# Agent attention and a top-1 mixture on one core: the first queries as f16 pairs among the keys, program order up to the first layer, and the last count of strays made early

## The chip, the cores and the metric

The kernel runs on one core of a Trainium2 chip. The metric is the device time of one execution in microseconds (us), from fast executions; the median of three runs stands for the kernel. One further execution was taken with a hardware profiler, and every row shown here comes from it. Engines are named as the profile names them: PE (matmuls), PEld (its weight loads), DVE (vector), ACT (scalar), POOL (GpSimd), SP (the queue that issues most DMAs).

## The reference

Attention through 49 agents per batch, then a mixture of 8 experts in which each token goes to the expert of its largest logit:

```python
# B, N, C = 4, 11456, 128; 49 agents; E, F = 8, 1024
a2k = softmax(scale * agents @ k.T)          # over the 11456 keys
agent_v = a2k @ v                            # 49 x 128
q2a = softmax(scale * q @ agents.T)          # over the 49 agents
x = (q2a @ agent_v).reshape(B * N, 128)

logits = normed(x) @ normed(expert_emb).T / tau
e = argmax(logits)
out = probs[e] * (relu(x @ w1[e]) @ w2[e])
```

Inputs and output are float32.

## The kernel before

**Units.** The tokens of a batch are laid out in 90 columns of (up to) 128. A unit is 8 columns: 128 partitions x 8 x 128 numbers, 512 KB, one load; a batch has 12 units (u = 0 to 11), the last of two columns of 96. Units of keys are kt, of values vt, of queries qt.

**The first batch's stages**, ahead of the first layer of the mixture:
- *Keys* (k1_f32). Each unit is transposed on PE in float32 (fTp, L362, 8 matmuls), copied out in halves by ACT and DVE (fT), multiplied with the agents (sp, L380, 8 matmuls, each run in two passes, 16 records), kept scaled as s_u by ACT (L383), and DVE keeps a running maximum m_run (L339).
- *Column maximum* (k_max, allmax): DVE reduces m_run to m, PE transposes it (mT, L149) and spreads the maximum (mB, L154), ACT copies it to pm.
- *Values* (k2_unit). DVE subtracts pm from s_u (kd, L398), ACT takes the exponential in place (L400), PE multiplies with the values (avp, L406), DVE adds up (avx, L412).
- *Fold and pick* (av_chain, pick_expert). PE folds the sums, the batch's main expert e0i is found (L487), SP reads it as a number (L545) and loads that expert's w1s and w2s (load_expert), which ACT and DVE turn into f16 pairs (gh, gl, w2h, w2l).

**Queries** (q_unit) need scores, DVE's maximum qmx and difference qe, ACT's exponential, and an f16 pair (high and low part) of the weights e that is transposed to tt; tt times r_hi and r_lo gives the router's sums (rtp), and tt feeds the mixture. Units 0 and 1 of the first batch are worked in float32 on PE (L566, and L588 for the transposes of e). All others go through split: ACT squares the unit for a scale (L299), DVE makes the scale out of it in three small operations (L179 to L183), ACT writes the high part (L303), POOL scales (L304) and subtracts for the low part (L305), SP issues a DMA transpose (L307), and PE takes 24 f16 matmuls (L316 to L318). Keys of later batches (k1_unit) go through split too.

**The mixture.** 736 steps (4 batches x 23 tiles x 8 slices of F): two matmuls of the first layer (hp, L723 and L724), ReLU and low part (hh on ACT, hl on DVE), twelve of the second (yp), then the output tile ot (L760). Beside it the next batch's keys and values and all queries are worked. Tokens whose expert is not e0 are strays: they are marked per batch, counted (count_strays: the maximum over partitions by mT, mB and pm, then running sums cum on DVE), and redone one group at a time. One group is redone beside the last batch (stray_first); at the end the count runs again, left over groups are computed (left, lefti), a register is loaded from lefti (L1097), and a loop runs over what is left.

**Order.** The generators run in rounds of a step counter, and each writes its instructions as it is reached; a number yielded is a wait in rounds. What the program writes is then placed by a scheduler on each engine, except that in the stages ahead of the first layer SP keeps the program's order (manual_schedule). k_max, av_chain and pick_expert run at high priority. In first, ops lists the units: 12 key units, two query units, the maximum, 12 value units, with two query units (u = 2, 3) and the next batch's first two key units set in between (BETWEEN); loads run AHEAD = 8 units ahead. Engine queues are in order: an instruction that waits holds up all behind it on its engine.

## Time and profile before

| what | value |
|---|---|
| runs | 1103.6, 1105.27, 1106.59 us (median 1105.27) |
| profiled execution | 1101.58 us, its span 1099.8 us |
| granted TensorE clock over the span | 0.973 of 2.4 GHz |
| PE busy | 1019.3 us, 93% of the span |
| DVE, ACT, POOL busy | 770.5, 724.2, 580.1 us |
| keys of the first batch | 0 to 46.6 us |
| maximum, first queries | 46.6 to 57.2 us |
| values | 57.2 to 84.25 us |
| fold, pick, weights | 84.25 to 101.2 us |
| mixture | 101.2 to 1094 us |
| count and end | 1094 to 1099.8 us |

Busy time is the union of an engine's instructions; an engine that is busy may still not be the one that sets the end. Start times count from the span's start. In a timeline row the bracket gives the idle time of the engine just before, and the instruction on whose end the idle time ended. A row of several instructions of the same kind ends in their count.

### The profile page before, as it was taken

To read this page: it belongs to the slowest core of one execution; us is meant where nothing else is said; L and a number is where in the kernel's file an instruction comes from. 1 tells how busy PE (TensorE), PEld (TensorE's weight loads), DVE (VectorE), ACT (ScalarE), POOL (GpSimd) and SP (SyncE) were. 2 spreads that over 40 slices of the span, in tenths; PEclk is the share of its full clock that TensorE was granted. 3 is DMA by queue.
4 is the path that set the end of the run, shared out by engine and by line. 5 is a ranking of instruction groups with operands and counts; after the bars stand their busy time and mean duration, and the time that the engine had idled before them with its cause. 6 is when DMAs were issued, how large, how long until landed. Compare 5 with 4: busy or idle time off the path is not lost.

```text
span 1099.8 us, 33877 instructions
## 1 busy us (share of the span) xinstructions
PE 1019.3 (93%) x13878; PEld 809.8 (74%) x13878; DVE 770.5 (70%) x1779; ACT 724.2 (66%) x1406; POOL 580.1 (53%) x653
## 2 busy tenths in 40 slices
PE   7876979999998898999999988999999989999997
PEld 7764767777776777777777766777777767877776
DVE  5665757666786677766686766766677778777785
ACT  3456978777559787766648866675556856755553
POOL 2334998786516987764524985544321835532300
PEclk9777999999999999999999999999999999999999
DMA  9549899956339988744436997452113524631101
GB/s 335 151 100 280 182 227 233 229 167 119 85 66 282 231 189 188 167 117 89 94 82 225 224 229 144 92 110 69 31 41 138 100 61 119 123 83 40 42 30 35
DMA packets 283944, 152.63 MB, mean 139 GB/s; under 512 B 208315, under 2 KB 260619, under 8 KB 283787
## 3 DMA queue, kind: packets, MB, share of 16 engines
q1 hardware_dynamic: 270603, 126.98, 51.2%
q10 hardware_dynamic: 13120, 23.47, 5.9%
q8 instruction: 109, 1.79, 0.7%
q14 instruction: 48, 0.39, 0.1%
q0 software_dynamic: 64, 0.00, 0.0%
HBM read 75.80 MB, written 23.53 MB: 90 GB/s over the span
## 4 chain that ended last, share of the span: by engine, by line
PE 53%; DMA 13%; POOL 13%; issue 9%; ACT 6%; DVE 5%; SPq 1%; ACTq 0%; POOLq 0%; DVEq 0%
PE hp L723 9%; PE yp L745 8%; PE yp L747 8%; PE hp L724 8%; PE yp L746 8%; DMA kT<-ks 4%; DMA tt<-e 4%; PE avp L406 4%; DMA qt<-in_q_dram 3%; POOL qs L305 2%; POOL qt L304 2%; POOL ks L305 2%; ACT hh L727 2%; POOL kt L304 2%; PE sp L380 2%
## 5 line engine op out<-in xcount | busy, mean ns | idle before, releaser
L728 DVE SCALAR_TENSOR_TENSOR hl<-hp,hh 128x512 f16<-128x512 f32 (+1 forms) x736 | 480.8, 671 | 142.5 <-ACT hh L727 121.7
L727 ACT ACTIVATE hh<-hp 128x512 f16<-128x512 f32 (+1 forms) x736 | 416.8, 588 | 186.1 <-PE yp L746 78.8
L745 PE MATMUL yp<-w2h,hh 128*128 128x128 f16 (+1 forms) x2880 | 522.4, 220 | 9.1 <-ACT hh L727 8.1
L746 PE MATMUL yp<-w2l,hh 128*128 128x128 f16 (+1 forms) x2880 | 521.7, 220 | 0.7 <-DVE w2l L532 0.7
L747 PE MATMUL yp<-w2h,hl 128*128 128x128 f16 (+1 forms) x2880 | 521.0, 220 | 0.0
L745 PEld LDWEIGHTS <-hh 128*128 128x128 f16 (+1 forms) x2880 | 285.3, 99 | 63.3 <-ACT hh L727 12.8
L747 PEld LDWEIGHTS <-hl 128*128 128x128 f16 (+1 forms) x2880 | 285.0, 99 | 47.2 <-issue 1.1
L746 PEld LDWEIGHTS <-hh 128*128 128x128 f16 (+1 forms) x2880 | 285.0, 99 | 42.1 <-issue 3.7
L723 PE MATMUL hp<-tt,gh 128*128 128x512 f16 (+1 forms) x736 | 275.9, 375 | 22.4 <-DVE hl L728 21.2
L724 PE MATMUL hp<-tt,gl 128*128 128x512 f16 (+1 forms) x736 | 276.0, 375 | 0.0
L304 POOL TENSOR_TENSOR qt<-qt,hsc 128x1024 f32<-128x1024 f32 (+1 forms) x46 | 81.8, 1781 | 49.6 <-ACT qs L303 42.9
L724 PEld LDWEIGHTS <-gl 128*128 128x128 f16 x736 | 72.0, 98 | 31.3 <-issue 28.7
L305 POOL TENSOR_TENSOR qs<-qt,qs 128x1024 f16<-128x1024 f32 (+1 forms) x46 | 92.0, 2004 | 0.4
L304 POOL TENSOR_TENSOR kt<-kt,hsc 128x1024 f32<-128x1024 f32 (+1 forms) x36 | 64.4, 1788 | 31.2 <-ACT ks L303 31.1
L723 PEld LDWEIGHTS <-gh 128*128 128x128 f16 x736 | 72.2, 98 | 8.5 <-issue 5.9
L650 POOL TENSOR_SCALAR l<-rtg 128x16 f32<-128x16 f32 (+2 forms) x28 | 8.2, 293 | 133.1 <-ACT rtg L615 132.4
L583 POOL TENSOR_TENSOR e<-qe,e 128x392 f16<-128x392 f32 (+1 forms) x46 | 39.7, 863 | 69.4 <-ACT e L582 58.7
L305 POOL TENSOR_TENSOR ks<-kt,ks 128x1024 f16<-128x1024 f32 (+1 forms) x36 | 72.8, 2022 | 0.6
L299 ACT ACTIVATE qs<-qt 128x1024 f16<-128x1024 f32 (+1 forms) x46 | 46.3, 1008 | 35.5 <-DMA qT<-qs 14.7
L648 POOL TENSOR_TENSOR nrm<-quad,half 128x16 f32<-128x16 f32 (+2 forms) x28 | 68.2, 2434 | 1.8
L406 PE MATMUL avp<-vt,kd 128*64 128x129 f32 x720 | 62.1, 297 | 6.5 <-issue 4.3
L760 DVE TENSOR_TENSOR ot<-yp,gs 128x512 f32<-128x512 f32 (+1 forms) x92 | 61.4, 670 | 9.6 <-PE yp L747 8.8
(264 smaller groups left out, 1452.7 us busy)
## 6 DMA issues: line engine op xcount, KB each, us to landing
kt<-in_k_dram SPq DMA_DIRECT2D x44, 512.0 KB, 5.9
qt<-in_q_dram SPq DMA_DIRECT2D x44, 512.0 KB, 6.2
vt<-in_v_dram SPq DMA_DIRECT2D x44, 512.0 KB, 5.2
out_dram<-ot ACTq DMA_DIRECT2D x88, 256.0 KB, 2.4
w1s<-in_moe_w_dram SPq DMA_DIRECT2D x5, 512.0 KB, 3.9
w2s<-in_moe_w_dram SPq DMA_DIRECT2D x5, 512.0 KB, 4.9
qT<-qs SPq DMA_TRANSPOSE x46, 5.0
tt<-e SPq DMA_TRANSPOSE x46, 3.5
```

The costliest lines, as they stand in the source:

```text
L304: pool.tensor_tensor(out=s[:p, :n], in0=s[:p, :n], in1=sc.unsqueeze(2).broadcast_to([p, n, D]), op=ALU.mult)
L305: pool.tensor_tensor(out=xs[:p, :n, 1], in0=s[:p, :n], in1=xs[:p, :n, 0], op=ALU.subtract)
L406: pe.matmul(out=avp[hs, :W], lhsT=de[:p, c * A : c * A + LO], rhs=src[:p, c, :], start=(c < 2), stop=(c >= n - 2), skip_group_check=True)
L648: pool.tensor_tensor(out=nrm, in0=quad[:, :n], in1=half[:, :n], op=ALU.pow)
L723: pe.matmul(out=hp[:, :m], lhsT=bt.gh[:, fs], rhs=tt, start=True, stop=False)
L724: pe.matmul(out=hp[:, :m], lhsT=bt.gl[:, fs], rhs=tt, start=False, stop=True)
L727: act.activation(hh[:, :m], hp[:, :m], AF.Relu)
L728: dve.scalar_tensor_tensor(out=hl[:, :m], in0=hp[:, :m], scalar=0.0, in1=hh[:, :m], op0=ALU.max, op1=ALU.subtract)
L745: pe.matmul(out=y, lhsT=hh[:, cs], rhs=bt.w2h[:, f, :], start=(f == 0 and c == 0), stop=False, skip_group_check=True)
L746: pe.matmul(out=y, lhsT=hh[:, cs], rhs=bt.w2l[:, f, :], start=False, stop=False, skip_group_check=True)
L747: pe.matmul(out=y, lhsT=hl[:, cs], rhs=bt.w2h[:, f, :], start=False, stop=last, skip_group_check=True)
L760: dve.tensor_tensor(out=o[:p, :n], in0=yp[:p, :n], in1=gate, op=ALU.mult)
```

## The change

It has five parts.
- **Queries 0 to 3 go through split**, among the keys: query unit 0 ahead of key unit 2, 1 ahead of 3, 2 ahead of 4, 3 ahead of 5 (QAT). The float32 way of the queries is gone. Weights e of all four are transposed by DMA (tt) and their low part is made by POOL.
- **In split, ahead of the mixture, the low part of a key unit** is one DVE operation in place of two on POOL, and there is a wait (5 rounds for queries, 1 for keys) ahead of the DMA transpose.
- **The next batch's key units 0 and 1** stand after value units 3 and 5 (KAT), not 8 and 11; AHEAD is 7; some waits in rounds are other numbers, and first also waits for these two units before av_chain.
- **Program order** up to the first layer holds for SP, PE, ACT and DVE, and high_priority is dropped there.
- **The last count of strays** with left and lefti is written in stray_first, as soon as the last batch is marked.

```diff
@@ split
-        pool.tensor_tensor(out=s[:p, :n], in0=s[:p, :n], in1=sc.unsqueeze(2).broadcast_to([p, n, D]), op=ALU.mult)
-        pool.tensor_tensor(out=xs[:p, :n, 1], in0=s[:p, :n], in1=xs[:p, :n, 0], op=ALU.subtract)
+        if kind == "k" and not ffn_at[0]:
+            dve.scalar_tensor_tensor(out=xs[:p, :n, 1], in0=s[:p, :n], scalar=sc, in1=xs[:p, :n, 0],
+                                     op0=ALU.mult, op1=ALU.subtract)
+        else:
+            pool.tensor_tensor(out=s[:p, :n], in0=s[:p, :n], in1=sc.unsqueeze(2).broadcast_to([p, n, D]), op=ALU.mult)
+            pool.tensor_tensor(out=xs[:p, :n, 1], in0=s[:p, :n], in1=xs[:p, :n, 0], op=ALU.subtract)
+        if not ffn_at[0]:
+            yield 5 if kind == "q" else 1
@@ q_unit
-        f32 = b == 0 and u < QF
-        if f32:
-            xT = pe_T(units["q", b, u], p, n)
...
-            iv = SCALE
-        else:
-            xT, iv = yield from split("q", b, u, g[0])
-            yield g[1]
-            spv = scores(b, u, xT)
+        xT, iv = yield from split("q", b, u, g[0])
+        yield g[1]
+        spv = scores(b, u, xT)
...
-        (dve if f32 else pool).tensor_tensor(out=e2[:p, :n, LO : LO + A], in0=e, in1=hi, op=ALU.subtract)
+        pool.tensor_tensor(out=e2[:p, :n, LO : LO + A], in0=e, in1=hi, op=ALU.subtract)
...
-        if f32:
-            tp = psh("tp").bitcast(F16)
-            for c in range(n):
-                pe.transpose(out=tp[:, c * p : (c + 1) * p], in_=e2[:p, c, :], identity=ident16[:p, :p])
-            act.copy(tt[:, : n * p], tp[:, : n * p])
-        else:
-            sp.dma_start_transpose(...)
+        sp.dma_start_transpose(...)
@@ stray_first
+        while not hasattr(batches[B - 1], "marked"):
+            yield 1
+        yield from count_strays()
+        dve.tensor_tensor(out=left, in0=cums[-1][:, NG - 1 :], in1=it, op=ALU.subtract)
+        dve.tensor_copy(lefti, left)
@@ first
-    BETWEEN = {1: ("q", 0, 2), 5: ("q", 0, 3), 8: ("k", 1, 0), 11: ("k", 1, 1)}
-    AHEAD = 8
+    QAT = {2: 0, 3: 1, 4: 2, 5: 3}
+    KAT = {3: 0, 5: 1}
+    AHEAD = 7
...
-                    spawn(k1_unit(b, u, (1, 6)))
+                spawn(k1_f32(b, u) if b == 0 else k1_unit(b, u, (1, 2)))
-                spawn(k2_unit(b, u, dve, (0, 1)))
+                spawn(k2_unit(b, u, dve, (0, 2)))
-                g = q_unit(b, u, (0, 1, 0, 0, 1, 0) if u < QF else (1, 6, 1, 1, 5, 1))
+                g = q_unit(b, u, (1, 2, 1, 0, 2, 0))
...
-        while batches[0].blks[0].k2 < NU or not ready:
+        while batches[0].blks[0].k2 < NU or not ready or batches[min(1, B - 1)].blks[0].k1 < NEXT:
             yield 1
-        with tc.high_priority():
-            now_run(av_chain(0, 0))
...
+        now_run(av_chain(0, 0))
@@ end of the kernel
-    with tc.manual_schedule(engines={mybir.EngineType.SP}):
+    with tc.manual_schedule(engines={ET.SP, ET.PE, ET.Activation, ET.DVE}):
...
-    now_run(count_strays())
-    left = sm.tile([P, 1], F32, name="left", tag="left")
-    lefti = sm.tile([P, 1], I32, name="lefti", tag="lefti")
-    dve.tensor_tensor(out=left, in0=cums[-1][:, NG - 1 :], in1=it, op=ALU.subtract)
-    dve.tensor_copy(lefti, left)
```

What that does to the engines' orders at the places that matter. PE before, at the end of the keys (e_0_151 is the pair of the first query unit's weights, m the column maximum, kd the values' weights):

```order
L588 LDWEIGHTS e_0_151
L588 MATMUL tp<-ident_137,e_0_151 128x128
L362 MATMUL fTp<-ident,qt 128x128 x5
L149 MATMUL mT<-ident,m_567 49x128
L362 MATMUL fTp<-ident,qt 128x128 x3
L154 MATMUL mB<-ident,mTx 128x49
L566 MATMUL sp<-aT_all,fT 128x49 x8
L406 MATMUL avp<-vt,kd_148 64x129 x8
```

PE now, at the same place (the lines are those of the changed kernel; L386 are the keys' scores, L322 to L324 a query's f16 scores):

```order
L324 LDWEIGHTS qT
L324 MATMUL sp<-a_132,qT 128x49
L386 MATMUL sp<-aT_all,fT 128x49 x8
L386 MATMUL sp<-aT_all,fT 96x49 x2
L149 MATMUL mT<-ident,m_676 49x128
L154 MATMUL mB<-ident,mTx 128x49
L322 LDWEIGHTS qT
L322 MATMUL sp<-a_132,qT 128x49
```

The maximum's transpose stands right behind the last keys; no transpose of weights is left, and the fourth query's scores follow mB.

PE now, in the middle of the keys, where the first query's scores begin (L368 are the keys' transposes):

```order
L368 MATMUL fTp<-ident,kt 128x128 x8
L386 MATMUL sp<-aT_all,fT 128x49 x8
L368 MATMUL fTp<-ident,kt 128x128 x16
L386 MATMUL sp<-aT_all,fT 128x49 x8
L368 MATMUL fTp<-ident,kt 128x128 x8
L322 LDWEIGHTS qT
L322 MATMUL sp<-a_132,qT 128x49
```

The first query group follows the eighth key unit's transposes and stands ahead of the seventh unit's scores.

SP's queue before, from the first DMA transposes to the register load of the expert's number:

```order
L114 DMA vt<-in_v_dram 128x8x128 x2
L307 DMA_TRANSPOSE qT<-qs 128x16x128
L114 DMA vt<-in_v_dram 96x2x128
L114 DMA kt<-in_k_dram 128x1024
L307 DMA_TRANSPOSE qT<-qs 128x16x128
L591 DMA_TRANSPOSE tt<-e_0_151 128x8x128
L307 DMA_TRANSPOSE kT<-ks 128x16x128 x2
L545 TENSOR_LOAD e0i
```

SP's queue now, first where the queries' transposes begin, then its end:

```order
L114 DMA kt<-in_k_dram 96x256
L114 DMA vt<-in_v_dram 128x8x128 x2
L313 DMA_TRANSPOSE qT<-qs 128x16x128
L114 DMA vt<-in_v_dram 128x8x128 x2
L313 DMA_TRANSPOSE qT<-qs 128x16x128
L114 DMA kt<-in_k_dram 128x1024
L581 DMA_TRANSPOSE tt<-e_0_151 128x8x128
```

```order
L581 DMA_TRANSPOSE tt<-e_0_151 128x8x128
L114 DMA kt<-in_k_dram 128x1024
L581 DMA_TRANSPOSE tt<-e_1_152 128x8x128
L114 DMA vt<-in_v_dram 128x8x128 x5
L114 DMA vt<-in_v_dram 96x2x128
L313 DMA_TRANSPOSE kT<-ks 128x16x128 x2
L551 TENSOR_LOAD e0i
```

All four queries' transposes now stand among the loads of values 0 to 5, those of the next batch's keys behind the last load of values; the register load still follows them.

DVE at the end now (hl belong to the mixture, L1090 is the register load):

```order
L718 SCALAR_TENSOR_TENSOR hl<-hp,hh 128x512
L925 TENSOR_TENSOR left<-cum,it 128x1
L926 CAST lefti<-left 128x1
L718 SCALAR_TENSOR_TENSOR hl<-hp,hh 128x512 x3
L750 TENSOR_TENSOR ot<-yp,gs 128x512
...
L718 SCALAR_TENSOR_TENSOR hl<-hp,hh 128x192 x3
L750 TENSOR_TENSOR ot<-yp,gs 96x256
L1090 TENSOR_LOAD lefti
```

Before, eleven operations from cum to lefti stood between the last ot and the register load; they have moved ahead of the last tiles.

## Rows read from the trace of the kernel before

**Rows 1.** Windows: start:end, length, busy PE, PEld, DVE, ACT, POOL, clock, DMA, GB/s
```profile
0.00:28.00 28.00, 21.06 (x161) 20.06 (x161) 16.20 (x43) 9.45 (x17) 6.24 (x30) 1.00 0.96 334
28.00:46.00 18.00, 16.43 (x127) 16.14 (x125) 12.52 (x35) 9.68 (x17) 6.79 (x9) 0.85 0.70 194
46.00:57.00 11.00, 7.19 (x35) 6.53 (x35) 4.85 (x11) 5.01 (x9) 2.24 (x3) 0.50 0.16 48
57.00:84.00 27.00, 20.35 (x229) 18.51 (x229) 17.81 (x33) 12.12 (x21) 9.20 (x7) 0.73 0.45 103
84.00:101.00 17.00, 9.62 (x113) 7.59 (x113) 7.11 (x34) 7.90 (x20) 4.63 (x9) 0.70 0.94 254
...
130.00:400.00 270.00, 252.95 (x3626) 196.56 (x3624) 188.62 (x454) 201.78 (x391) 195.59 (x195) 0.99 0.81 185
```

**Rows 2.** The chain of waits up to 140 us: start, length, what (xcount)
```profile
21.96 0.89 PE fTp L362 x8
22.85 1.72 PE sp L380 x16
...
46.67 3.66 PE sp L566 x16
```

**Rows 3.** Fine windows of PE alone: start:end, length, busy PE, clock, DMA, GB/s
```profile
38.00:38.50 0.50, 0.00 (x0) 1.00 1.10 326
...
41.00:41.50 0.50, 0.50 (x4) 0.50 1.05 292
...
64.50:65.00 0.50, 0.50 (x12) 1.00 1.61 184
```

**Rows 4.** Timeline, 46 to 58 us: start, length, engine, line, operation, out<-in, shapes [idle before]
```profile
47.07 0.82 DVE L418 TENSOR_REDUCE m<-m_run 128x49 f32<-128x392 f32 x1
...
53.36 1.03 PE L588 MATMUL tp<-ident,e 128*128 128x128 f16 x8 [3.04 <-DVE e L583]
...
55.25 0.42 PE L149 MATMUL mT<-ident,m 128*49 128x128 f32 x1
...
57.17 1.76 DVE L398 TENSOR_TENSOR kd<-s_u,pm 128x392 f32<-128x392 f32 x1
```

**Rows 5.** Timeline, POOL and DVE passes, 33 to 37.5 and 103 to 106 us
```profile
34.67 1.89 POOL L304 TENSOR_TENSOR qt<-qt,hsc 128x1024 f32<-128x1024 f32 x1 [1.02 <-ACT qs L303]
...
36.64 2.12 POOL L305 TENSOR_TENSOR qs<-qt,qs 128x1024 f16<-128x1024 f32 x1
36.79 1.99 DVE L242 TENSOR_TENSOR emb_n<-xc,yr 8x1 f32<-8x1 f32 x1
...
103.75 1.36 DVE L532 SCALAR_TENSOR_TENSOR w2l<-w2s,hsc,w2h 128x1024 f16<-128x1024 f32 x1 [0.86 <-ACT w2h L529]
```

**Rows 6.** Timeline, ACT in the value stage
```profile
70.76 1.06 ACT L299 ACTIVATE ks<-kt 128x1024 f16<-128x1024 f32 x1 [3.12 <-DMA kt<-in_k_dram]
```

**Rows 7.** DMA issues: what, queue, xcount, median us to landing (60:66, then 84.5:92 us)
```profile
qT<-qs SPq DMA_TRANSPOSE x1, 7.2
...
kT<-ks SPq DMA_TRANSPOSE x2, 4.7
```

**Rows 8.** Timeline, PE: the first and the last of a query unit's 24 score matmuls
```profile
77.88 0.22 PE L316 MATMUL sp<-a,qT 128*128 128x49 f16 x1
...
78.57 0.18 PE L318 MATMUL sp<-a,qT 128*128 128x49 f16 x1
```

**Rows 9.** The chain of waits from 84 us, and the timeline's first matmul of the mixture
```profile
87.83 0.16 DVE e0i L487
...
89.93 0.75 SPq L545
...
101.19 0.38 PE L723 MATMUL hp<-tt,gh 128*128 128x512 f16 x1
```

**Rows 10.** Timeline, DVE at the end
```profile
1093.92 0.42 DVE L760 TENSOR_TENSOR ot<-yp,gs 96x256 f32<-96x256 f32 x1 [0.61 <-PE yp L747]
...
1096.11 0.15 DVE L1096 CAST lefti<-left 128x1 int32<-128x1 f32 x1
```

More of the change, by code (lines that the diff above doesn't have):

```diff
@@ L559, in q_unit @@
             yield 1
-        f32 = b == 0 and u < QF
-        if f32:
-            xT = pe_T(units["q", b, u], p, n)
-            yield 1
-            s = pss("sp")
-            for c in range(n):
-                pe.matmul(out=s[:p, c * A : (c + 1) * A], lhsT=xT[:, c * p : (c + 1) * p], rhs=aT_all[:, b, :], start=True, stop=True)
-            spv = s[:p, : n * A].rearrange("p (c a) -> p c a", a=A)
-            iv = SCALE
-        else:
-            xT, iv = yield from split("q", b, u, g[0])
-            yield g[1]
-            spv = scores(b, u, xT)
+        xT, iv = yield from split("q", b, u, g[0])
+        yield g[1]
+        spv = scores(b, u, xT)
         mx = sm.tile([P, UJ], F32, name="qmx", tag="qmx")[:p, :n]
@@ L582, in q_unit @@
         act.copy(hi, e)
-        (dve if f32 else pool).tensor_tensor(out=e2[:p, :n, LO : LO + A], in0=e, in1=hi, op=ALU.subtract)
+        pool.tensor_tensor(out=e2[:p, :n, LO : LO + A], in0=e, in1=hi, op=ALU.subtract)
         tt = wk.tile([P, UJ * P], F16, name="tt", tag="tt", bufs=LEAD + 2)
-        if f32:
-            tp = psh("tp").bitcast(F16)
-            for c in range(n):
-                pe.transpose(out=tp[:, c * p : (c + 1) * p], in_=e2[:p, c, :], identity=ident16[:p, :p])
-            act.copy(tt[:, : n * p], tp[:, : n * p])
-        else:
-            sp.dma_start_transpose(out=tt[:, : n * p].rearrange("k (c p) -> k c p", p=p),
-                                   in_=e2[:p, :n, :].rearrange("p c k -> p (c k)"))
+        sp.dma_start_transpose(out=tt[:, : n * p].rearrange("k (c p) -> k c p", p=p),
+                               in_=e2[:p, :n, :].rearrange("p c k -> p (c k)"))
         yield g[4]
@@ L769 @@
     cums = []
+    left = sm.tile([P, 1], F32, name="left", tag="left", bufs=1)
+    lefti = sm.tile([P, 1], I32, name="lefti", tag="lefti", bufs=1)
     def count_strays():
@@ L955, in run_step @@
         run_half()
-    QF = 2
-    BETWEEN = {1: ("q", 0, 2), 5: ("q", 0, 3), 8: ("k", 1, 0), 11: ("k", 1, 1)}
-    NEXT = sum(x[0] == "k" for x in BETWEEN.values()) if B > 1 else 0
-    AHEAD = 8
+    QAT = {2: 0, 3: 1, 4: 2, 5: 3}
+    KAT = {3: 0, 5: 1}
+    NEXT = len(KAT) if B > 1 else 0
+    AHEAD = 7
     def first():
-        ops = [("k", 0, u) for u in range(NU)] + [("q", 0, u) for u in range(QF)] + [("m", 0, 0)]
+        ops = []
+        for u in range(NU):
+            if u in QAT:
+                ops.append(("q", 0, QAT[u]))
+            ops.append(("k", 0, u))
+        ops.append(("m", 0, 0))
         for u in range(NU):
             ops.append(("v", 0, u))
-            if u in BETWEEN and BETWEEN[u][1] < B:
-                ops.append(BETWEEN[u])
+            if u in KAT and B > 1:
+                ops.append(("k", 1, KAT[u]))
         X = {"k": k, "v": v, "q": q}
@@ L982, in first @@
                     k_start(b)
-                if b == 0:
-                    spawn(k1_f32(b, u))
-                else:
-                    spawn(k1_unit(b, u, (1, 6)))
+                spawn(k1_f32(b, u) if b == 0 else k1_unit(b, u, (1, 2)))
             elif kind == "v":
-                spawn(k2_unit(b, u, dve, (0, 1)))
+                spawn(k2_unit(b, u, dve, (0, 2)))
             elif kind == "q":
-                g = q_unit(b, u, (0, 1, 0, 0, 1, 0) if u < QF else (1, 6, 1, 1, 5, 1))
+                g = q_unit(b, u, (1, 2, 1, 0, 2, 0))
                 if u == 0:
@@ L999, in first @@
                     yield 1
-                with tc.high_priority():
-                    now_run(k_max(0, psh, 0))
+                now_run(k_max(0, psh, 0))
             yield 1
-        while batches[0].blks[0].k2 < NU or not ready:
+        while batches[0].blks[0].k2 < NU or not ready or batches[min(1, B - 1)].blks[0].k1 < NEXT:
             yield 1
-        with tc.high_priority():
-            now_run(av_chain(0, 0))
-            now_run(q0[0])
-            q0[0] = iter(())
-            now_run(batches[0].pick)
+        now_run(av_chain(0, 0))
+        now_run(q0[0])
+        q0[0] = iter(())
+        now_run(batches[0].pick)
     def keys():
@@ L1066 @@
     spawn(first())
-    with tc.manual_schedule(engines={mybir.EngineType.SP}):
+    ET = mybir.EngineType
+    with tc.manual_schedule(engines={ET.SP, ET.PE, ET.Activation, ET.DVE}):
         while not hasattr(batches[0], "iall"):
```

## The prediction

> **What bounds the kernel now.** I read the stage windows first: in each row the third number group is the busy time of PE, the one before the DMA share is the granted clock of TensorE in full speeds, 0.50 being 1.2 GHz of 2.4. From 130 us on PE works 253 of 270 us at 0.99 [rows 1]: that stretch is bound by TensorE, and the change takes nothing out of it. The hundred microseconds ahead of the first layer are the place: five windows, all with PE idle in part, three of them at 0.73 or less. The chain of waits gives the price of a key unit there: its 8 float32 transposes (T) 0.89 us, its 16 score passes (S) 1.72 us, and an S at the low clock 3.66 us [rows 2].
>
> Then the fine windows. PE stands still at 38.0 to 38.5, a little later it is busy all the time at 0.50, and it is back at 1.00 at 64.5, in the dense passes over the values [rows 3]. The standstill has a cause in the timeline: a DVE operation on 8x1 numbers takes 1.99 us while POOL's second pass over a query unit runs, and DVE's running maximum, for which PE waits, is behind it [rows 5]. What the low clock cost: 28 to 46 us has a mean of 0.85, so 0.15/0.5 = 30% of 18 us, 5.4 us, ran at half speed and lost 2.7 us.
>
> Last the end of the keys: the maximum over columns starts at 47.07, but its transpose mT runs at 55.25, because the transposes of the first query's weights (L588) stand ahead of it in PE's queue and wait for DVE until 53.36. The first difference kd of the value stage starts at 57.17 [rows 4]. I measure all that follows by the start of kd.
>
> **Keys stage, with the queries in it.** What goes: 2 T of queries (2x0.89), two S at the low clock (2x3.66), the L588 transposes, and the wait above. What comes: four f16 score groups of 24 matmuls; one takes 78.75-77.88 = 0.87 us as the clock rises, of which the second half runs at full speed, so I take 0.7 each [rows 8]. The queries' POOL passes cost 1.89+2.12 = 4.0 us a unit [rows 5] and run one after the other. Walked by hand along the new order: ACT has scaled q0 at an estimated 19.25 (behind the scaled scores of the first two key units), POOL is done with q0 at 23.3 and with q1 at 27.4. SP's queue has q0's DMA transpose behind the load of v1, and that load waits for the buffer that POOL frees with q1; so the transpose issues at 28. Transposes landed 4.7 and 7.2 us after issue [rows 7]: q0's scores can start between 32.7 and 35.2, I take 33.5. PE's order puts them behind the eighth T. Before, the sixth S ends two steps of T and S after the fourth (22.85+2x2.61+1.72 = 29.8 [rows 2]); the same six S stand ahead of q0 now, so PE is there at about 29.9 and waits 3.6 us (2.8 to 5.3). Queued behind that wait are all remaining S, T, and through them DVE's maxima. After it come S of six units, five whole and one of two columns (5x1.72+0.43 = 9.0), T of four (3x0.89+0.22 = 2.9) and three query groups (2.1): 14.0, with 0.8 of short waits S ends at 48.3. The column maximum (0.82 [rows 4]) ends at 49.9; mT to kd took 57.17-55.25 = 1.9 [rows 4], and q3's maximum and difference now stand on DVE ahead of kd (1.1 by estimate from two passes of about 0.56): with PE's q3 group between, kd starts at 53.3. **-3.9 us** at full clock.
>
> **The clock after the q0 wait.** The wait is a standstill like that of 38 us, but twice as long; then the clock fell though PE was busy again. I take that it falls and comes back in the mixed stream of T, S and query groups, and price it as the nearest row, the 2.7 us lost between 28 and 46 [rows 1, 3]: **+2.7**, bounds 0 (no fall) and +14.0 (all 14.0 us of the rest at half speed).
>
> **Value stage.** Before 57.17 to 84.25, 27.1 us. POOL's passes over the two key units of the next batch go to one DVE operation each (1.36 us, as w2l [rows 5]), ahead of whose end their transposes can't issue. ACT's square of such a unit stood before with 3.12 us of idle ACT time for its load, with the exponentials queued behind it [rows 6]; the loads now issue among the queries' transposes, far earlier, so that wait goes. In its place PE, now in program order, has the scores of k(1,0) behind the sixth value unit and of k(1,1) behind the ninth. Each waits for SP's transpose and 4.7 us of landing [rows 7]; the values behind it wait too, and DVE's accumulation and the free buffers with them. Walked with no loss of clock the stage takes 26.7 us, with both waits at the low clock 30.8: -0.4 to +3.7. I take **+0.7**: the loads are early and PE has six units to run ahead of the first wait.
>
> **The expert's load.** SP read e0i at 89.93, though DVE had it at 87.83+0.16 = 87.99: the two kT transposes stood ahead [rows 9]. They stand ahead still, but their scores now precede v9, so they are long out. That frees 1.9 us; ACT's program order puts the square of the next key unit between the two parts of the weights' work, one square of 1.06 us [rows 6], of which I let 0.7 count: **-1.2** (-1.9 to 0). The first matmul of the first layer, 101.19 before [rows 9], is the sum of all this.
>
> **The tail.** Before, the last ot ends at 1094.34, then DVE counts until lefti ends at 1096.26, and the register load follows [rows 10]. Now left and lefti are made some tiles earlier, and the load follows ot: **-1.9** (-1.5 if the last output's transfer ends later than that). The early count's small DVE passes, two PE and one ACT operations lie between FFN tiles; if the PE transpose there waits for the last mark, it costs what it waits, under 0.5 by the spacing of such passes.
>
> The FFN keeps its operations; its order on DVE and POOL differs for about the first quarter. I take 0, bounds -3 and +3: PE idles 17 us of the 270 there [rows 1], and a sixth of that may move either way.
>
> **Sum**: -3.9+2.7+0.7-1.2-1.9 = -3.6. The profiled run took 1101.58 us (span 1099.8), the median of the three runs is 1105.27. From the run to 1098.0, and with the same 3.7 us to the median: **1101.7**. About 0.3%, 3.3 us, is what can be told from no change here.
>
> **Rivals.**
> - Clock kept. If q0 lands early, or PE comes later than I think, the wait is short and 2.7 is not lost: -6.3, 1099.0. For it: the transposes' landing of 4.7 was the case with an idle queue. Against: DMA is 96% busy in the first 28 us [rows 1].
> - Clock lost for the rest of the keys, the case slower than before. Place: PE at the query group q0. Price: 14.0 us of work at half speed, +14.0 in place of +2.7, so -3.6+11.3 = +7.7, 1113.0. It decides when the stream behind q0 does not bring the clock back before the last S; break-even with before is at 6.3 us lost, when 45% of that work runs slow. For it: from 46 to 57 us every window is at 0.50, and S passes without a gap at 41.0 did not lift it [rows 1, 3]. Against: the stream now has T and f16 groups in it, and dense avp did lift it by 64.5.
> - Order on PE. Both kT waits at their full 30.8: +3.7 in place of +0.7, total -0.6, 1104.7.
> - FFN order: +3 in place of 0, total -0.6, or -3 to 1098.7.
>
> The Trainium skill, page "TensorE: Matmul & The Clock Gate", section "Part 1: The HAM clock gate", says that throttled is the default and that activity releases it. By that rule alone the gapless stream behind q0 would bring the clock back, and the sum would stay at the forecast or the first rival. The trace agrees at 64.5 only: at 41.0 a PE without gaps was at 0.50, so being busy was not enough there.
>
> **How the numbers follow.** Forecast 0.36 (half of it beyond 3.3 us); clock kept 0.27, all but 0.01 faster; clock lost 0.15, slower; order on PE 0.16 (0.11 same, 0.05 slower with some clock loss); FFN 0.06 (0.03 faster, 0.01 same, 0.02 slower). Faster: 0.18+0.26+0.03 = 0.47. Slower: 0.15+0.05+0.02 = 0.22, and 0.02 of the forecast with the clock later than thought: 0.24. Same: 0.29. The range goes from 1095 (clock kept, value stage at -0.4, FFN -3: 1094.9) to 1112, just short of the full loss of clock, where a tenth is left out.
>
> **What would show it.** PE's first query group: an idle stretch of 3 to 5 us ending near 33.5, and granted clock below 1.00 behind it. kd's start near 56 (53.3 to 54 if the clock holds, over 62 if it is lost). No 3 us of idle ACT ahead of a square in the value stage, but PE waiting ahead of the scores from kT. The register load of e0i within 0.3 us of e0i. The last ot followed by a register load, and the end some 3.5 us behind it. I am wrong if kd starts earlier than 53, which would mean a shorter wait than any row allows, or if the first layer starts earlier than 94.

## The result

The changed kernel takes 1121.24 us (median of four runs, 1114.95 to 1123.92) against 1105.93 for the kernel before: a ratio of 1.0134, interval 1.0087 to 1.0180. It is 1.3% slower, where 1101.7 and a gain were forecast. The profiled execution took 1120.08 us, its span 1118.3 against 1099.8. The 18.5 us lie here, by the starts of four instructions in both traces (kd, the fold's first matmul foldp, the first and the last matmul of the first layer hp):

| stretch | before, us | after, us | difference | forecast |
|---|---|---|---|---|
| start to the first kd | 57.17 | 66.13 | +9.0 | -1.2 (-3.9 and +2.7) |
| kd to the fold | 27.08 | 31.88 | +4.8 | +0.7 |
| fold to the first hp | 16.94 | 17.93 | +1.0 | -1.2 |
| first hp to the last hp | 989.9 | 994.2 | +4.3 | 0 |
| last hp to the end | 8.7 | 8.2 | -0.5 | -1.9 |

The stage windows of the changed kernel (start:end, length, busy PE, PEld, DVE, ACT, POOL, clock, DMA share, GB/s), which answer to [rows 1]:

```profile
0.00:28.00 28.00, 22.13 (x102) 21.00 (x102) 12.72 (x41) 11.43 (x18) 10.77 (x29) 1.00 0.76 284
28.00:46.00 18.00, 17.21 (x138) 16.77 (x138) 9.38 (x19) 9.97 (x17) 12.62 (x13) 1.00 0.93 205
46.00:57.00 11.00, 8.39 (x103) 8.20 (x101) 5.39 (x12) 3.48 (x8) 0.91 (x1) 0.83 0.94 192
57.00:84.00 27.00, 13.36 (x136) 11.82 (x135) 11.44 (x39) 11.02 (x20) 2.27 (x8) 0.63 0.83 184
84.00:101.00 17.00, 11.55 (x146) 10.05 (x147) 7.48 (x22) 4.79 (x9) 0.00 (x0) 0.80 0.17 32
...
130.00:400.00 270.00, 251.12 (x3562) 195.65 (x3561) 188.29 (x452) 200.50 (x385) 195.49 (x191) 0.98 0.78 175
```

PE is as busy in the first 28 us as before, but does 102 records there and not 161. The clock column says 1.00; it can't be trusted there: the record holds changes only, and the first one, in this run at 36.3 us, is a rise, so nothing is on record ahead of it. The durations tell the level. PE's timeline of the changed kernel (start, length, line, operation, count):

```profile
8.68 1.92 PE L368 MATMUL fTp<-ident,kt 128*128 128x128 f32 x8
...
11.04 7.07 PE L386 MATMUL sp<-aT_all,fT 128*128 128x49 f32 x32
17.90 1.93 PE L368 MATMUL fTp<-ident,kt 128*128 128x128 f32 x8
19.66 3.65 PE L386 MATMUL sp<-aT_all,fT 128*128 128x49 f32 x16
...
33.52 3.27 PE L368 MATMUL fTp<-ident,kt 128*128 128x128 f32 x16
36.63 1.88 PE L386 MATMUL sp<-aT_all,fT 128*128 128x49 f32 x16
...
54.21 0.22 PE L322 MATMUL sp<-a,qT 128*128 128x49 f16 x1 [2.61 <-DMA qT<-qs]
...
55.21 4.27 PE L386 MATMUL sp<-aT_all,fT 128*128 128x49 f32 x20
```

T takes 1.93 and S 3.65 us, twice what [rows 2] show: PE is at 1.2 GHz from its first matmul to 36 us. The rise comes in the two T that stand together at 33.52. The one wait for a query's transpose is q2's, 2.61 us at 54.2; the clock falls again in it, at 53.3, and the last 20 records of S take 4.27 us. The first kd, then in the value stage the transposes of the next batch's key units in SP's queue, and PE's waits ahead of their scores:

```profile
66.13 0.55 DVE L404 TENSOR_TENSOR kd<-s_u,pm 128x392 f32<-128x392 f32 x1
...
79.25 11.45 SPq L313 DMA_TRANSPOSE kT<-ks  x2
...
84.50 0.22 PE L322 MATMUL sp<-a,kT 128*128 128x49 f16 x1 [6.15 <-DMA kT<-ks]
...
93.04 0.20 PE L322 MATMUL sp<-a,kT 128*128 128x49 f16 x1 [1.77 <-DMA kT<-ks]
```

Behind the fold, ACT (and PE's first layer, last row):

```profile
110.76 1.06 ACT L299 ACTIVATE ks<-kt 128x1024 f16<-128x1024 f32 x1 [3.03 <-DMA kt<-in_k_dram]
...
111.81 1.40 ACT L527 ACTIVATE gh<-gp,sgw 128x256 f16<-128x256 f32 x3
...
115.94 0.61 PE L713 MATMUL hp<-tt,gh 128*128 128x512 f16 x1
```

The square of the next batch's third key unit stands in ACT's queue ahead of gh and waits 3.03 us for its load; sgw, which gh needs, was ready at 109.1, so gh starts 2.7 us late.

### The profile page after: what moved, and what is told of

The parts are those of the page before. It is cut to its first block, busy times and chain, and to the rows that moved or that the text cites. A ratio compares the mean times of both kernels' runs of the same rounds, so it can differ in the third digit from the quotient of the medians.

```text
span 1118.3 us, 33832 instructions
## 1 busy us (share of the span) xinstructions
PE 1025.7 (92%) x13862; PEld 813.8 (73%) x13862; DVE 761.9 (68%) x1783; ACT 726.9 (65%) x1408; POOL 581.9 (52%) x655
## 4 chain that ended last, share of the span: by engine, by line
PE 48%; DMA 15%; POOL 12%; issue 8%; ACT 6%; DVE 3%; SPq 1%; ACTq 0%; POOLq 0%
PE hp L713 8%; PE hp L714 8%; PE yp L735 8%; PE yp L737 8%; PE yp L736 8%; DMA kT<-ks 6%; PE avp L412 4%; DMA tt<-e 3%; DMA qt<-in_q_dram 2%; POOL qt L308 2%; POOL qs L309 2%; DMA kt<-in_k_dram 2%; POOL ks L309 2%; POOL kt L308 2%; ACT hh L717 2%
## 5 line engine op out<-in xcount | busy, mean ns | idle before, releaser
L308 POOL TENSOR_TENSOR qt<-qt,hsc 128x1024 f32<-128x1024 f32 (+1 forms) x48 | 85.7, 1787 | 64.9 <-ACT qs L303 52.5
L309 POOL TENSOR_TENSOR qs<-qt,qs 128x1024 f16<-128x1024 f32 (+1 forms) x48 | 96.4, 2012 | 0.6
L714 PEld LDWEIGHTS <-gl 128*128 128x128 f16 x736 | 72.0, 98 | 30.8 <-issue 28.8
L308 POOL TENSOR_TENSOR kt<-kt,hsc 128x1024 f32<-128x1024 f32 (+1 forms) x34 | 60.7, 1784 | 31.5 <-ACT ks L303 31.5
L309 POOL TENSOR_TENSOR ks<-kt,ks 128x1024 f16<-128x1024 f32 (+1 forms) x34 | 68.3, 2008 | 0.6
L299 ACT ACTIVATE qs<-qt 128x1024 f16<-128x1024 f32 (+1 forms) x48 | 48.4, 1008 | 30.8 <-DMA kT<-ks 14.1
```

What stands on the lines that cost most here:

```text
L308: pool.tensor_tensor(out=s[:p, :n], in0=s[:p, :n], in1=sc.unsqueeze(2).broadcast_to([p, n, D]), op=ALU.mult)
L309: pool.tensor_tensor(out=xs[:p, :n, 1], in0=s[:p, :n], in1=xs[:p, :n, 0], op=ALU.subtract)
L714: pe.matmul(out=hp[:, :m], lhsT=bt.gl[:, fs], rhs=tt, start=False, stop=True)
```

## The experiments

Two theories at first: the start at the low clock is the cause of the late keys (theory 1), or it goes along with a loss in the order (theory 2). The abbreviations T (a unit's float32 transposes) and S (its score passes) go on. Later sections ask for the value stage, the tail and the mixture. The ratio of each version is taken to runs of the kernel before on the same chip. The medians of these are 1105.9 beside the changed kernel and 1101.9 to 1103.1 beside all others, so versions are compared by their ratios. Start of the first kd, first hp, and the time from the first to the last hp come from one trace of each kernel. The trace of a_keyslate is of an execution 10 us above its median. The first 180 rows of PE's order (all of the keys) are the same in the changed kernel, a_katlate, a_keyslate and a_nokat.

| kernel | median, us | ratio (interval) | first kd | fold | first hp | first to last hp |
|---|---|---|---|---|---|---|
| before | 1105.9 | | 57.2 | 84.3 | 101.2 | 989.9 |
| after | 1121.2 | 1.0134 (1.0087 to 1.0180) | 66.1 | 98.0 | 115.9 | 994.2 |
| a_warm | 1120.4 | 1.0141 (1.0102 to 1.0181) | 64.8 | 97.3 | 115.5 | 999.1 |
| b_warm | 1097.3 | 0.9943 (0.9913 to 0.9973) | 53.7 | 78.1 | 93.9 | 995.3 |
| a_tfirst | 1110.3 | 1.0080 (1.0049 to 1.0110) | 58.9 | 90.6 | 108.0 | 988.3 |
| a_sponly | 1110.0 | 1.0087 (1.0051 to 1.0122) | 63.0 | 91.4 | 106.4 | 988.5 |
| a_alt | 1119.3 | 1.0159 (1.0111 to 1.0208) | 62.8 | 95.3 | 114.2 | 994.0 |
| a_alt_warm | 1124.5 | 1.0179 (1.0124 to 1.0235) | 67.8 | 100.4 | 119.2 | 997.8 |
| a_alt_q4 | 1117.1 | 1.0110 (1.0067 to 1.0152) | 51.2 | 84.0 | 102.9 | 1005.3 |
| a_katlate | 1136.0 | 1.0315 (1.0266 to 1.0365) | 65.7 | 99.8 | 119.6 | 1005.4 |
| a_nokat | 1121.6 | 1.0166 (1.0126 to 1.0206) | 61.6 | 80.6 | 98.8 | 1006.9 |
| a_keyslate | 1126.3 | 1.0192 (1.0123 to 1.0261) | 76.1 | 108.0 | 124.5 | 1002.3 |
| b_manual | 1135.0 | 1.0276 (1.0226 to 1.0326) | 56.6 | 101.9 | 118.2 | 1003.4 |
| b_count | 1102.1 | 0.9980 (0.9959 to 1.0000) | 57.1 | 83.9 | 102.6 | 990.8 |
| a_alt_q4_kdve | 1116.0 | 1.0140 (1.0103 to 1.0178) | 51.7 | 84.4 | 103.2 | 999.2 |
| b_kdve | 1115.5 | 1.0096 (1.0066 to 1.0126) | 57.1 | 82.4 | 98.9 | 1012.4 |
| b_count_warm | 1095.4 | 0.9930 (0.9910 to 0.9950) | 54.2 | 77.8 | 95.3 | 993.0 |
| b_kdve_count_warm | 1108.0 | 1.0049 (1.0029 to 1.0069) | 54.6 | 76.3 | 93.2 | 1005.6 |
| a_alt_q4_klater | 1129.2 | 1.0232 (1.0203 to 1.0261) | 57.4 | 91.1 | 109.7 | 1013.2 |
| b_count_warm_klater | 1112.3 | 1.0096 (1.0072 to 1.0120) | 52.4 | 76.4 | 94.4 | 1008.3 |

### A warm start

a_warm (on the changed kernel) and b_warm (on the kernel before):

```diff
+    warm = cst.tile([P, 512], F16, name="warm")
+    pool.memset(warm, 0.0)
+    w_ = psy("warmp")
+    with tc.manual_schedule(engines={mybir.EngineType.PE}):
+        for _ in range(16):
+            pe.matmul(out=w_, lhsT=warm[:, :P], rhs=warm, start=True, stop=True)
```

> The changed kernel with 16 f16 matmuls of 128x512 on zeros, whose result nobody reads, ahead of PE's first transposes, where PE stood idle. Theory 1 (the changed order leaves PE at 1.2 GHz from 6.7 to 36 us, since only two key units' transposes stand ahead of the score passes): the clock rises before 10 us, a step of one T and one S takes 2.6 us and not 5.2, the value stage begins at 54 to 59 us and not at 66.1, and the kernel gains 7 to 12 us on the changed one: 1109 to 1114. Theory 2 (the keys are late for another reason in the order, the clock only goes along): T and S become shorter, but the value stage still begins at 64 or later and the gain is under 3 us.

> The kernel before with the same 16 matmuls ahead of PE's first transposes: what a warm start is worth where the clock rose at 13.3 us anyway. Theory 1: three units of transposes at half the time, 1 to 3 us gained at the start, total 1102 to 1105. Theory 2: no change, 1104 to 1108.

The timeline of a_warm (PE), then its windows (start:end, length, busy PE, clock, DMA share, GB/s):

```profile
7.19 1.97 PE L374 MATMUL fTp<-ident,kt 128*128 128x128 f32 x16
...
11.50 6.33 PE L392 MATMUL sp<-aT_all,fT 128*128 128x49 f32 x32
```

```profile
12.00:13.00 1.00, 1.00 (x9) 0.67 1.02 418
13.00:14.00 1.00, 1.00 (x6) 0.50 1.00 410
...
36.00:37.00 1.00, 1.00 (x11) 0.88 0.85 179
```

Two T now take 1.97 together: the clock is up. Then PE stands still for 1.15 and 0.37 us around the first maximum, the two S begin, and at 12.3 the clock is gone, while PE is busy without a gap, until 36.2, as in the changed kernel. So a_warm settled neither theory, but it showed that the start of the changed order did not keep a clock that was up. In b_warm, where six units of T follow with gaps under 0.3 us, the clock was up from 5.2 to 35.9, and 5 us were gained, more than the 1 to 3 expected.

### More transposes ahead of the scores

a_tfirst makes four units' T ahead of the first S; a_sponly leaves PE, ACT and DVE to the scheduler, which puts three T there.

```diff
-        yield 2
+        yield {0: 6, 1: 6, 2: 4, 3: 3}.get(u, 2)
```

```diff
-    with tc.manual_schedule(engines={ET.SP, ET.PE, ET.Activation, ET.DVE}):
+    with tc.manual_schedule(engines={ET.SP}):
```

> The changed kernel with the first four key units' transposes ahead of the first scores (the wait between a unit's transposes and its scores is 6, 6, 4, 3 rounds for the first four units and 2 for the others), and nothing else. Theory 1: the transposes stand together as in the kernel before, the clock rises by 14 us, and the value stage begins at 55 to 60 us: 1109 to 1115. Theory 2: the same work in another order, no gain over 3 us.

> The changed kernel with only SP in program order ahead of the first layer; PE, ACT and DVE are placed by the scheduler, as in the kernel before. Three key units' transposes stand ahead of the first scores. Theory 1: the clock rises by 14 to 18 us, and the value stage begins by 60: 1108 to 1115. Theory 2 (program order itself is the loss, in all stages): the keys and the value stage are both shorter, total 1100 to 1108.

PE's timeline of a_tfirst, then of a_sponly:

```profile
13.71 6.08 PE L386 MATMUL sp<-aT_all,fT 128*128 128x49 f32 x48
19.59 1.93 PE L368 MATMUL fTp<-ident,kt 128*128 128x128 f32 x8
```

```profile
11.81 3.77 PE L386 MATMUL sp<-aT_all,fT 128*128 128x49 f32 x32
15.42 1.06 PE L368 MATMUL fTp<-ident,kt 128*128 128x128 f32 x8
```

In a_tfirst the clock rose at 11.8, and fell at 18.6 in three S that stand together; in a_sponly it rose at 10.1 and stood through two S, to 34.0. Their first hp comes 8.0 and 9.5 us earlier than in the changed kernel, the one in program order on PE, ACT and DVE and the other not. The ratio falls from 1.0134 to 1.0080 and 1.0087; the intervals overlap, so the gain in the total, some 5 us, is less sure than the one in the traces. Theory 1 held in the keys, with a_sponly's first kd (63.0) behind its forecast (by 60): PE waits there for DVE's running maximum (4.21 us ahead of the S at 44.62). No loss from program order as such is seen at this place.

### Transposes and scores in turn

```diff
-        yield 2
+        kb.t = u + 1
+        while kb.t < min(u + 3, NU):
+            yield 1
```

> The changed kernel with one edit: a key unit's scores follow the transposes of the second unit behind it, so that PE takes one T and one S in turn from the third T on, and no two S stand together until the last units. Theory 1a (two S in a row drop the clock, and T and S in turn keep whichever level they meet; the warm matmuls rose the clock at 5.5 and the pair S, S lost it at 12.3): the clock rises by 10 to 14 us and holds until PE first stands still, the value stage begins at 53 to 58, total 1104 to 1111. Theory 1b (the mix itself can't hold the clock): it falls again within 7 us of the first S, the value stage begins at 60 or later, 1111 to 1120.

> As a_alt, with the 16 matmuls on zeros ahead of the first transposes. Theory 1a: the clock is up at 5.5 and holds through the first S; value stage at 51 to 56, total 1102 to 1108. Theory 1b: as a_warm, which lost the clock at 12.3: value stage at 60 or later.

a_alt, PE's timeline and windows:

```profile
8.68 1.55 PE L368 MATMUL fTp<-ident,kt 128*128 128x128 f32 x8
...
23.58 1.05 PE L368 MATMUL fTp<-ident,kt 128*128 128x128 f32 x8
30.87 0.22 PE L322 MATMUL sp<-a,qT 128*128 128x49 f16 x1 [6.24 <-DMA qT<-qs]
```

```profile
26.00:27.00 1.00, 0.00 (x0) 0.90 2.37 248
27.00:28.00 1.00, 0.00 (x0) 0.50 1.28 56
43.00:44.00 1.00, 1.00 (x12) 0.57 1.13 338
```

The clock rises at 9.7 and stays up with T and S in turn: a step takes 2.6 us. The rise comes in the second T (1.55 us), when PE has done just what it did in the changed kernel up to that point (8.68 there too, 1.92 us). So two T in front were enough here, as in b_manual and a_nokat below (10.7), and were not in the changed kernel. The order ahead of the first S doesn't settle, then, whether the clock rises there, and what does stays open. a_nokat, which has the changed kernel's order, shows what the order behind it does: two S follow, and the clock falls at 14.1 in them.

The faster start has a price. PE is at the first query group at 24.6, and now the wait that the prediction spoke of is there, 6.24 us. The clock falls in it and stays at 0.50 until 43.9, though PE is busy. In the changed kernel the slow start had hidden this wait: PE came to q0 at 39.2 and did not wait. With that, a_alt's first kd (62.8, forecast 53 to 58) and total missed theory 1a's forecast. a_alt_warm lost the clock at 14.7, behind two waits of 1.30 and 0.86 us at the start, much like a_warm, and had the warm matmuls for nothing; its forecast was missed too.

a_alt_q4 moves the query groups' scores two units back:

```diff
-                g = q_unit(b, u, (1, 2, 1, 0, 2, 0))
+                g = q_unit(b, u, (1, 4, 1, 0, 2, 0))
```

> As a_alt, with one number more changed: four rounds and not two between a query unit's transposes and its scores, so that PE's first query group stands behind the tenth key unit's transposes and not the eighth's. In a_alt PE waited 6.24 us for q0's transposes, to 30.87, and the clock fell at 26.8 and stayed low to 43.9. Theory 1c (the wait for q0 is what loses the clock in the keys once the start is warm): the wait is 0 to 2.5 us, the clock stays up to 35 or later, the value stage begins at 52 to 58 (62.8 in a_alt), total 1105 to 1114. Rival (the clock falls in that stretch for any reason): value stage at 61 or later, total 1116 to 1122.

PE's timeline of a_alt_q4, the first query group, and DVE's first kd:

```profile
30.47 0.20 PE L322 MATMUL sp<-a,qT 128*128 128x49 f16 x1 [0.47 <-DMA qT<-qs]
...
51.19 0.56 DVE L406 TENSOR_TENSOR kd<-s_u,pm 128x392 f32<-128x392 f32 x1
```

The wait is 0.47 us, the clock holds to 37.3, the first kd starts at 51.19, 11.6 us earlier than in a_alt and 6.0 earlier than before the change. The keys are settled by that. The total is not (1117.1, where 1105 to 1114 was expected): its value stage takes 32.8 us, 27.1 before the change, and its mixture 1005 us, 990 before and 994 in the changed kernel.

### The value stage

a_katlate has KAT = {8: 0, 11: 1}, a_nokat has KAT = {} and no wait for these two units ahead of the fold (they are worked in the mixture).

> The changed kernel with the next batch's key units 0 and 1 behind value units 8 and 11, as before the change; all else is the change. If the value stage's 31.8 us come from PE standing ahead of these units' scores (6.15 and 1.77 us), the waits move behind the last value units: from the first kd to the fold 25 to 28 us, but a wait of 3 to 8 us ahead of the fold or of the expert's load takes some of it back, since the fold follows these scores in program order. Total 1114 to 1122. If it comes from the clock in that stage alone: 30 us or more still.

> The changed kernel with no key unit of the next batch in the first stages (they are worked beside the mixture with the ten others); the rest is the change. Theory (the value stage is 31.8 us long since PE stands ahead of these units' scores): from the first kd to the fold 23 to 27 us; the mixture has two more key units beside it, 0 to 2 us; total 1112 to 1118. Rival (the clock, or DVE's kd, makes the stage long): 29 us or more.

PE's timeline of a_katlate at the end of its value stage, then a_nokat: two S at the start on PE, and its value stage as one window (all engines):

```profile
89.29 0.22 PE L322 MATMUL sp<-a,kT 128*128 128x49 f16 x1 [2.98 <-DMA kT<-ks]
...
98.80 0.22 PE L322 MATMUL sp<-a,kT 128*128 128x49 f16 x1 [8.33 <-DMA kT<-ks]
```

```profile
10.91 4.15 PE L386 MATMUL sp<-aT_all,fT 128*128 128x49 f32 x32
```

```profile
61.60:80.60 19.00, 14.32 (x181) 12.41 (x181) 9.83 (x37) 8.15 (x14) 1.02 (x2) 0.81 0.44 106
```

Without the two units the stage takes 19.0 us and not 31.9, with them at the end 34.1 (25 to 28 was expected), 11.3 of it waits for their transposes ahead of the fold. So these units cost 13 us in that stage, their work and the lower clock included (mean 0.72 in the changed kernel's stage, 0.81 in a_nokat's), and the waits are longest where nothing is left to work on. How much of it is PE's program order wasn't isolated: a_sponly, where the scheduler places PE with the same two units in the stage, takes 28.4. And a_nokat's first layer, 2.4 us earlier than before the change, brought nothing: its mixture took 1006.9, and its total missed its forecast.

### The weights, the tail, and program order alone

a_keyslate starts the later batches' keys two rounds later (spawn(keys(), 2)). b_count puts the early count alone into the kernel before. b_manual is the kernel before with SP, PE, ACT and DVE in program order.

> The changed kernel with the generator of the later batches' keys started two rounds later, so that on ACT no square of such a unit stands between the two parts of the first weights' work (gh). Theory: ACT stood 3.03 us for that unit's load with gh behind it; from e0i to the first matmul of the first layer then 11.5 to 12.5 us and not 14.8; the total falls by about 3, within what the clock scatters (1113 to 1121). Rival (the first layer waits for something else as well, w2 or the routers' sums): 14 us or more still.

> The kernel before with the early last count alone (part 5 of the change). The prediction's step: 1.9 us less. By the trace of the changed kernel, where the end comes 5.1 us behind the last ot and came 5.5 us behind it before: 0.4 us less. Medians within 1 us of the kernel before would say the second.

> The kernel before with SP, PE, ACT and DVE in program order up to the first layer, and nothing else: two units of transposes, not three, stand ahead of the first scores, and from there T and S come in turn. If program order is what leaves the start at the low clock: no rise before 30 us, a step of T and S at 5.2 us, value stage 5 to 12 us later than before, 1108 to 1118. If it is the queries among the keys: the clock rises by 14 us, and the total is 1097 to 1106.

In a_keyslate's trace (1136.6 us) the clock first rose at 80.7, so only its order is read here, on ACT:

```profile
119.80 0.47 ACT L527 ACTIVATE gh<-gp,sgw 128x256 f16<-128x256 f32 x1 [1.45 <-DVE sgw L520]
```

gh now waits for sgw alone, no square is ahead of it, and from e0i to the first hp it is 12.7 us, not 14.8. The theory of ACT's queue held in the main, with 2.1 of the 3.0 us (11.5 to 12.5 was expected).

b_count, the last ot (the end of its span is at 1100.41), and the changed kernel's (1118.31):

```profile
1096.12 0.42 DVE L760 TENSOR_TENSOR ot<-yp,gs 96x256 f32<-96x256 f32 x1 [0.96 <-PE yp L747]
```

```profile
1112.80 0.42 DVE L750 TENSOR_TENSOR ot<-yp,gs 96x256 f32<-96x256 f32 x1 [0.96 <-PE yp L737]
```

From the last ot's start to the end it was 5.88 us before [rows 10], is 4.29 in b_count, and 5.51 in the changed kernel. Alone, the count gives 1.6 in the trace, near the prediction's 1.9, where I expected 0.4; the medians differ by 0.6 and can't tell the two apart. In the changed kernel it gave 0.4. The transfers there show one of 16 KB on the instruction queue that starts 0.8 us behind ot's end; in b_count it starts ahead of ot. All sixteen traces with the early count divide that way: in ten it starts 0.8 to 1.1 us behind ot's end, and from the last ot to the end it is 5.0 to 5.5 us; in six it starts ahead of that end, and it is 3.9 to 4.3. a_warm, whose edit is at the start alone, goes from the changed kernel's 5.51 to 3.88, with that transfer 0.8 us ahead. So a load of instructions most likely takes back what the count gives, though no run moves this load alone.

b_manual's first kd is at 56.6, its clock up from 10.7 to 44.8. Program order alone therefore doesn't leave the start at the low clock, even with two T at the start; T and S come in turn there. Its trace is 30.5 us longer than the one of before; 17.0 of that are lost by the first hp, all in the value stage, 45 us long, and 13.4 in the mixture. The value stage:

```profile
62.90 1.99 PE L406 MATMUL avp<-vt,kd 128*64 128x129 f32 x16 [1.56 <-issue]
...
66.56 1.99 PE L406 MATMUL avp<-vt,kd 128*64 128x129 f32 x16 [1.68 <-issue]
```

PE pauses about 1.6 us or more behind nearly every unit there (16 records, 1.99 us, the lower clock): 41.5 us from the first unit to the twelfth. In that time the units go one by one: DVE's kd of a unit starts behind avx of the unit before (61.58 behind 61.37), the exponential follows on ACT (62.18), then PE.

### What the mixture gives back

a_alt_q4's first hp is at 102.9, 1.7 us later than before; at the 24th of 736 steps it is 4.8 behind, at the 47th 15.4 (by hp's starts), 13.7 lost on the way. Its two windows around that (all engines), then PE's timeline:

```profile
130.00:160.00 30.00, 29.20 (x446) 22.70 (x444) 22.88 (x55) 27.24 (x53) 29.84 (x28) 1.00 1.14 213
160.00:190.00 30.00, 17.36 (x253) 14.36 (x253) 14.81 (x38) 19.54 (x34) 28.19 (x21) 0.77 1.12 234
```

```profile
166.27 0.23 PE L592 MATMUL rtp<-r_hi,tt 128*128 128x58 f16 x1 [4.29 <-DMA tt<-e]
...
177.96 0.26 PE L737 MATMUL yp<-w2h,hh 128*128 128x128 f16 x1 [5.03 <-DVE ot L752]
```

PE waits for a query's transposed weights, then for an output tile, whose gate hangs on them; POOL is busy 28 of 30 us. So POOL was the suspect, though it is busy 29.8 of 30 us in the window ahead of that, where PE loses little. a_alt_q4_kdve and b_kdve take the second batch's keys off it, to one DVE operation a unit; b_kdve_count_warm and b_count_warm stand beside them:

```diff
-        if kind == "k" and not ffn_at[0]:
+        if kind == "k" and (not ffn_at[0] or b == 1):
```

> a_alt_q4 with the second batch's key units split by one DVE operation and not two on POOL, beside the mixture too. Theory (POOL's load in the mixture's first 90 us holds PE: its passes for keys stand ahead of those for queries and gates): the loss of 12 us between step 0 and step 46 goes to 5 or less, the total to 1103 to 1110. Rival (SP's and PE's queues hold it, POOL is only busy): loss 9 us or more, total 1113 to 1120.

> The kernel before with the same edit, in the mixture only. Theory: PE idles 7 us less in its first 100 us of mixture, 1096 to 1101. Rival: DVE's 1.3 us passes stand ahead of hl, for which PE waits, and eat it: 1100 to 1106.

> The kernel before with the early count and the 16 matmuls on zeros ahead of the transposes. The warm start alone gave 1097.3 against 1102.5, the early count alone 0.6: 1096 to 1099 if they add up, 1100 to 1104 if the warm start's gain was an accident of its order.

> The kernel before with all three edits. If POOL bounds the mixture's first stretch, the earlier start is kept: 1090 to 1096. If not, as b_count_warm: 1096 to 1101.

The same window in a_alt_q4_kdve:

```profile
130.00:160.00 30.00, 23.36 (x326) 17.28 (x324) 24.30 (x52) 21.78 (x40) 14.42 (x15) 0.94 1.12 275
```

POOL is busy 14.4 of 30 us, and PE still loses 11 us, only earlier, ahead of the 24th step. b_kdve made the kernel before 1% slower, and b_kdve_count_warm came out at 1108.0; both lie above every time that was expected. So to relieve POOL alone is no cure. That POOL's load costs nothing is not shown by it, since the edit loads DVE in its place: in a_alt_q4_kdve PE waits 9.9 us for hl between 103 and 190 us, in a_alt_q4 4.2. Last, the second batch's keys later, so that the queries come first:

```diff
-        W_ = [(0, 0.25, 0.3, 0.8), ...
+        W_ = [(0.08, 0.3, 0.35, 0.8), ...
```

> a_alt_q4 with the keys of the second batch spread over steps 15 to 55 of the mixture, not 0 to 46. Theory (transposes and loads of keys, in order on SP ahead of the queries' ones, hold the gates for which the output tiles wait): the loss of 12 us between step 0 and step 46 falls to 6 or less, and the total to 1103 to 1111. Rival (any order but the one of the kernel before loses about as much): 9 us or more, 1112 to 1120.

> b_count_warm with the same edit. Theory: PE's idle time around 150 us (some 5 us) shrinks, 1090 to 1095. Rival: the order in the mixture was the good one, 1096 to 1108.

Both lost, and lie above every time that was expected: the loss between the first and the 47th step grew to 15.5 us in the one and came up new, 14.4, in the other. So that theory's forecast failed too. Before, b_warm, b_count and b_count_warm have the same order on POOL and SP in the mixture's first part, but for a few neighbours that change places, and take 990 to 995 us from the first to the last hp. Of the sixteen others, whose order differs there, eleven take 999 to 1013 and five 988 to 998. Others that share an order lie together as well: the changed kernel and a_tfirst 994 and 988, a_alt, a_alt_warm and a_warm 994 to 999, a_alt_q4 and a_katlate 1005 both, b_kdve and b_kdve_count_warm 1012 and 1006. That the order makes the difference is argued from this, and no run tries it alone; which of the queues (SP's transposes, POOL, ACT, the gates) sets it stays open. A few microseconds between single traces mean little: runs of the kernel before alone spread from 1097.1 to 1107.1 us.

b_count_warm is the fastest version: 1095.4 us, 0.9930 of the kernel before (0.9910 to 0.9950). b_warm, at 0.9943, is faster than both kernels as well.

## Why the prediction was wrong

- **The step that failed is the clock at the start.** The walk took S and T at 1.72 and 0.89 from the first steps on, as in [rows 2], where the clock was up at 13.3. But [rows 2] hold for a start with three units of T together; the changed order has two, then two S. No row of before shows that start, and I bounded the clock only behind the wait for q0. The first two S took 7.07 us (3.77 in a_sponly) and the three steps of T and S from 17.9 to 33.5 15.6 in place of 7.8: the sixth S ended at 38.5 and not at 29.8, and q0's scores started at 39.2 and not at 33.5. a_tfirst and a_sponly, with more T in front, have the first hp 8.0 and 9.5 us earlier. Why the clock rose behind the first two T in a_alt, b_manual and a_nokat and not in the changed kernel stays open; in a_nokat, with the same order, it fell again at 14.1 in the two S.
- **Behind q0** the walk had 19.8 us to kd, 22.5 with the 2.7 for the clock; it took 26.9. The fall of the clock came, but at q2's transpose, whose wait of 2.61 us no term named, and the last 20 records of S took 4.27 us in place of 2.15.
- **The wait for q0** was right as a mechanism and at the wrong time. With the clock up (a_alt) it is 6.24 us, ending at 30.87, where 3.6 (2.8 to 5.3) ending at 33.5 was written; PE came earlier than 29.9. There the clock came back in the mixed stream, as written, but after 17.1 us (26.8 to 43.9) and not after the 5.4 that the price was taken from. The rival "clock lost" put 14.0 us on the clock behind it; a_alt against a_alt_q4 shows 11.6 at the first kd, with the wait itself (5.8 us of difference) in it. In the changed kernel itself it didn't occur.
- **The keys without a lost clock** were undersold: kd at 53.3 by the walk, 51.19 in a_alt_q4, whose order differs a little. The walk's terms don't quite add up either: 48.3 and 0.82 are 49.1 and not 49.9 (the last running maximum, 0.64 us before the change, isn't named), and 49.9, 1.9 and 1.1 are 52.9 and not 53.3.
- **The value stage** was mis-sized: 31.9 us against a walk of 26.7 to 30.8, of which I took 27.8. The two waits on kT were named, but not that their cost is not the landing alone: DVE's scale and ACT's square come behind the exponentials, so kT(1,0) was issued only at 79.25, with PE dry from 78.4. The two units together cost 13 us in the stage by a_nokat, of which 7.9 are PE's two waits.
- **The expert's load**: from e0i to w1s's issue it is 1.5 us and not 3.3, 1.8 gained as written. The square of a key unit on ACT was counted at 0.7 by its own length; it waits 3.03 us for its load, and gh, behind it, starts 2.7 us late (2.1 by a_keyslate).
- **The tail**: 1.6 when alone, 0.4 in the change, most likely for the load of instructions. (Twelve small DVE operations moved, not eleven.)
- **The mixture** was given 0 with bounds of 3; +4.3 here by one trace each, which their scatter could make, but 15 us in a_alt_q4. What starts earlier must not be booked as gained where a scheduler makes the order behind it anew.

What stands of the rivals: "clock lost" named the right resource and the wrong place, and its 1113.0 fell short by 8, because the value stage and, as far as one trace tells, the mixture lost too.

What the prediction cites from the Trainium skill, page "TensorE: Matmul & The Clock Gate", section "Part 1: The HAM clock gate", that activity releases the throttle, doesn't agree with this trace: PE was busy without a gap from 6.7 to 33 us and stayed at the lower level (S 3.65 us). The measurement decides. The prediction's own row for it, 41.0 us before the change, lies 0.4 us behind the fall of the clock at 40.6 and shows little by itself.

## What to carry to other kernels

An order on TensorE has a price at either clock level, so look first at what the new order puts at the start and behind each wait, and read the level from durations where the record of the clock has not begun. In program order an instruction that waits for a transfer costs all that is behind it, so place it by when the transfer lands, and count with the fast case: a gain upstream brings PE earlier to the same transfer. A gain ahead of a long stage has to be followed through that stage's own order before it is booked.

## What the runs showed of the hardware

- PE busy is not the clock held. T and S in turn kept the level that they met, 1.00 in a_alt to 24.6 us and 0.50 in the changed kernel for 15 us. The clock fell in three S that stand together in a_tfirst (18.6) and in two in a_nokat (14.1), and stood through two S in a_sponly. It rose in two T that stand together (36.3 in the changed kernel) and, before the change, in the avp matmuls (64.5).
- The clock's record begins at the first change; 1.00 ahead of that is not a reading (T 1.93 against 0.89 us).
- With the same PE order in the keys, the clock's lasting rise came at 36.3 (after), 36.4 (a_katlate) and 34.6 us (a_nokat, which had it from 10.7 to 14.1 too), and the first kd at 66.1, 65.7 and 61.6. The clock rose in or right behind the first two T in a_alt (9.7), b_manual (10.7) and a_nokat (10.7), and not in the changed kernel: one trace of an order doesn't tell the level that the next execution starts at.
- The end of the program came 3.9 to 4.3 us behind the start of the last ot where a transfer of 16 KB on the instruction queue started ahead of ot's end (six traces), and 5.0 to 5.5 where it started 0.8 to 1.1 us behind it (ten traces).
